# FFN2 of chunks 1 to 8 as a seven-product block multiplication, in an attention-plus-FFN kernel

## The chip, the cores and the metric

One core of one Trainium2 chip. The metric is device time in microseconds (us) of one execution, the median of several; lower is better. Before the change: 338.33 us (337.58 to 338.6, three runs). The profiled executions have a span some 2 us shorter than the timed value, because the span runs from the first to the last instruction.

## The reference, cut to what matters

```python
def reference(q, k, v, w_gate, w_val, w_out):            # shortened
    # q, k, v: 8 batches, 8 heads, 576 positions, head size 64
    attn = softmax(q k^T / 8, masked to |i-j| <= 32) v
    x = attn as [4608 tokens, 512]
    g = x @ w_gate                                       # 512 -> 1536
    val = x @ w_val
    return (g * sigmoid(g) * val) @ w_out                # 1536 -> 512, float32
```

The last line is FFN2, the two lines ahead of it are FFN1. The kernel works through the tokens in nine chunks of 512. Only FFN2 of chunks 1 to 8 is changed.

## The kernel before

FFN1 of a chunk is twelve units. A unit is eight matmuls of 512 columns into one of two `gv_ps` buffers (in PSUM, where matmuls put their results), a silu on ScalarE, and a multiply on VectorE that writes a row of blocks of hT and frees the buffer.

```python
    def ffn1_unit(j, fk):
        ...
        gv = ps_a.tile([128, 2, 512], FP32, tag="a", name="gv_ps")     # ps_a: 2 buffers
        for i, w in enumerate((wg16, wv16)):
            for g in range(GS):
                nc.tensor.matmul(out=gv[:, i, :], lhsT=w[:, g, 128 * fk:128 * fk + 128],
                                 rhs=xts[j][:, g, :], start=(g == 0), stop=(g == GS - 1))
        ssb = spool.tile([128, 512], FP16, tag="s", name="ssb")
        nc.scalar.activation(out=ssb, in_=gv[:, 0, :], func=AF.Silu, bias=0.0, scale=1.0)
        nc.vector.tensor_tensor(out=hts[j][:, fk, :], in0=ssb, in1=gv[:, 1, :], op=ALU.mult)

    def ffn2_sub(j, sub, half=None):                     # 128 tokens, half of the contraction
        ...
        for fk in {None: range(FKS), 0: range(FKS // 2), 1: range(FKS // 2, FKS)}[half]:
            nc.tensor.matmul(out=ob, lhsT=hts[j][:, fk, 128 * sub:128 * sub + 128],
                             rhs=wo16[:, fk, :], start=(fk == 0), stop=(fk == FKS - 1))
        if half == 0:
            return
        osb = opool.tile([128, d_model], FP32, tag="osb", name="osb")
        nc.scalar.activation(out=osb, in_=ob, func=AF.Copy, bias=0.0, scale=1.0)
        nc.sync.dma_start(out=out[r0:r0 + 128, :], in_=osb)
```

FFN2 of a chunk has eight slots (four times 128 tokens, two halves). The attention of the next batch is woven between them, in pieces of 128 tokens (two blocks of 64) that the program calls pairs: scores with exp (ScalarE) and mask (VectorE), then the product with v, a division on VectorE that gives x, and a transpose transfer that gives xT, which FFN1 of the next chunk needs.

```python
        groups = {1: ((), (0, 1)), 3: ((0,), (2, 3)), 5: ((1, 2), (4,)), 7: ((3, 4), ())}
        for slot in range(8):
            at_a, at_s = groups.get(slot, ((), ()))
            done = [todo[i] for i in at_a if i < n]
            for i, m in enumerate(done):
                pair_av(m, ps_a if i else None)          # o_ps on PE, then x on VectorE
            for i in at_s:
                if i < n:
                    pair_scores(todo[i])                 # s_ps on PE, exp on ScalarE, mask on VectorE
            for m in done:
                pair_xt(m)                               # transpose transfer of x
            ...
            ffn2_sub(j, slot // 2, slot % 2)
```

The last 128 tokens of chunk 8 go through `ffn2_last`, in two halves of 256 columns, so that the last output transfer is small.

## Time and profile before

I call the time from the first FFN2 matmul of chunk j to the first FFN1 matmul of chunk j+1 "stage j".

| | us |
|---|---|
| time, median | 338.33 |
| FFN1 of a chunk | 20.7 to 20.9 |
| FFN2 of chunk 7, nothing woven in | 10.36 |
| stages 1 to 6, attention woven in | 13.3 to 14.7 |
| last FFN2 matmul to the end | 5.76 |

The page of the kernel before, its first part (busy time and share of the span by engine), two rows of its second part (busy tenths in 40 equal slices) and its fourth part (the chain of work that ended last):

```profile
span 336.5 us, 6449 instructions
PE 321.8 (96%) x2592; PEld 154.4 (46%) x2592; DVE 157.5 (47%) x289; ACT 155.6 (46%) x222; POOL 106.3 (32%) x139
...
PE   5789998999999999999999999999999999999993
...
DVE  3743366337624763466345644564446634404400
...
PE 87%; DMA 4%; ACT 3%; DVE 3%; issue 1%; SPq 1%; ACTq 0%
PE gv_ps L392 56%; PE ob L406 24%; PE o_ps L354 3%; PE s_ps L306 3%; DMA qk_st<-in_k_dram 2%; DMA xT<-x 2%; ACT xT L262 1%; ACT p_t L312 1%; DVE x L363 1%; PE qk_ps L281 1%; DVE p_t L344 1%; PE ob L425 1%; ACT v L262 1%; SPq L215 0%; PE warm L438 0%
```

TensorE (PE) is the bound from the fifth slice on, so fewer columns through it should be less time. VectorE (DVE) looks half idle.

The groups of instructions of the kernel before, one line for each shape. The columns are line, engine, operation, output and inputs, shapes, count; then busy us and mean ns of one; then the idle time of the engine just before them and what ended it:

```profile
L406 PE MATMUL ob<-wo,hT 128*128 128x512 f16 x420 | 97.3, 380 | 0.0
L399 DVE TENSOR_TENSOR hT<-ssb,gv_ps 128x512 f16<-128x512 f16 x108 | 74.3, 688 | 122.5 <-ACT ssb L398 122.1
L322 DVE TENSOR_TENSOR p_t<-p_t,mask 128x1024 f16<-128x1024 f16 x32 | 22.0, 691 | 14.4 <-ACT p_t L312 14.3
L425 PE MATMUL ob<-wo,hT 128*128 128x256 f16 x24 | 2.8, 272 | 0.0
```

The "380" and "272" are modelled lengths of pipelined matmuls; the pitch is what counts, 216 ns for 512 columns and 109.6 ns for 256 (24 of them in 2.63 us in the chain).

Two more views of the kernel before are needed later. First, who TensorE waited for ahead of FFN1 (line, whom for, us in total, times, longest):

```profile
PE gv_ps L392 <- ACT xT L262: 1.1, 2, 0.7
PE gv_ps L392 <- DMA xT<-x: 0.8, 2, 0.6
```

### The profile page before, as it was taken

How to read it: one execution, taken by the hardware profiler on the slowest of the kernel's cores; microseconds unless marked ns; L12 is line 12 of the kernel's file. 1: busy time of each engine (PE TensorE's matmuls, PEld its weight loads, DVE VectorE, ACT ScalarE, POOL GpSimd, SP SyncE). 2: the span in 40 equal slices, each digit the busy share in tenths (PEclk: the TensorE clock that was granted, in tenths of full speed). 3: DMA queues.
4: the chain of work that ended last, by engine and by line, in shares of the span. 5: the costliest groups of instructions: out<-in, count | busy, mean ns of one | idle time of the engine just before them, and what ended most of it. 6: DMA issues, size and time to landing. Idle time of an engine off the chain costs nothing.

```text
span 336.5 us, 6449 instructions
## 1 busy us (share of the span) xinstructions
PE 321.8 (96%) x2592; PEld 154.4 (46%) x2592; DVE 157.5 (47%) x289; ACT 155.6 (46%) x222; POOL 106.3 (32%) x139
## 2 busy tenths in 40 slices
PE   5789998999999999999999999999999999999993
PEld 2444554444544454445444454454445544444442
DVE  3743366337624763466345644564446634404400
ACT  3864577434543474338333843373337443223321
POOL 8972776148004620364047302560000000000000
PEclk9999999999999999999999999999999999999998
DMA  7999999999959996999599958995530420020012
GB/s 278 161 204 302 217 164 190 153 137 123 128 141 139 112 149 134 131 134 127 158 121 143 117 132 116 153 139 127 120 62 33 111 63 0 34 94 0 2 63 71
DMA packets 152981, 41.92 MB, mean 125 GB/s; under 512 B 140528, under 2 KB 146416, under 8 KB 152944
## 3 DMA queue, kind: packets, MB, share of 16 engines
q0 software_dynamic: 100640, 16.52, 67.2%
q1 hardware_dynamic: 52304, 24.92, 30.6%
q8 instruction: 22, 0.36, 0.5%
q14 instruction: 15, 0.12, 0.1%
HBM read 37.75 MB, written 9.44 MB: 140 GB/s over the span
## 4 chain that ended last, share of the span: by engine, by line
PE 87%; DMA 4%; ACT 3%; DVE 3%; issue 1%; SPq 1%; ACTq 0%
PE gv_ps L392 56%; PE ob L406 24%; PE o_ps L354 3%; PE s_ps L306 3%; DMA qk_st<-in_k_dram 2%; DMA xT<-x 2%; ACT xT L262 1%; ACT p_t L312 1%; DVE x L363 1%; PE qk_ps L281 1%; DVE p_t L344 1%; PE ob L425 1%; ACT v L262 1%; SPq L215 0%; PE warm L438 0%
## 5 line engine op out<-in xcount | busy, mean ns | idle before, releaser
L399 DVE TENSOR_TENSOR hT<-ssb,gv_ps 128x512 f16<-128x512 f16 x108 | 74.3, 688 | 122.5 <-ACT ssb L398 122.1
L398 ACT ACTIVATE ssb<-gv_ps 128x512 f16<-128x512 f32 x108 | 64.5, 597 | 113.2 <-PE gv_ps L392 110.8
L392 PE MATMUL gv_ps<-xT,wg 128*128 128x512 f16 x432 | 110.8, 379 | 1.8 <-ACT xT L262 1.1
L392 PE MATMUL gv_ps<-xT,wv 128*128 128x512 f16 x432 | 110.9, 379 | 0.0
L406 PE MATMUL ob<-wo,hT 128*128 128x512 f16 x420 | 97.3, 380 | 0.0
L392 PEld LDWEIGHTS <-wg 128*128 128x128 f16 x432 | 41.9, 98 | 52.3 <-issue 3.4
L392 PEld LDWEIGHTS <-wv 128*128 128x128 f16 x432 | 42.3, 98 | 51.0
L406 PEld LDWEIGHTS <-hT 128*128 128x128 f16 x420 | 38.5, 98 | 43.7
L223 POOL DMA_DIRECT2D tok<-in_q_dram x30 | 25.2, 841 | 82.0 <-DMA qT<-tok 79.0
L312 ACT ACTIVATE p_t<-s_ps 128x1024 f16<-128x1024 f32 (+1 forms) x40 | 35.4, 935 | 11.2 <-PE s_ps L306 11.1
L414 ACT ACTIVATE osb<-ob 128x512 f32<-128x512 f32 x35 | 21.0, 599 | 39.6 <-PE ob L406 39.6
L223 POOL DMA_DIRECT2D tok<-in_k_dram x30 | 25.2, 839 | 18.7 <-DMA kT<-tok 13.4
L322 DVE TENSOR_TENSOR p_t<-p_t,mask 128x1024 f16<-128x1024 f16 x32 | 22.0, 691 | 14.4 <-ACT p_t L312 14.3
L363 DVE TENSOR_TENSOR x<-o_ps,rall 128x512 f16<-128x512 f32 x36 | 24.9, 692 | 1.2
L242 POOL DMA_DIRECT2D v<-in_v_dram x24 | 21.5, 906 | 0.3 <-PE s_ps L306 0.3
L265 DVE COPY v<-v 64x512 f16<-64x512 f16 x54 | 18.4, 341 | 1.7
L354 PEld LDWEIGHTS <-p_t 128*64 128x64 f16 x576 | 11.2, 110 | 10.4 <-issue 5.9
L354 PE MATMUL o_ps<-v,p_t 128*64 128x66 f16 x576 | 14.0, 196 | 0.7 <-DVE p_t L344 0.7
L361 DVE RECIPROCAL rall<-o_ps 128x8 f32<-128x8 f32 x36 | 7.3, 203 | 14.8 <-PE o_ps L354 14.8
L306 PE MATMUL s_ps<-qT,kT 64*128 64x64 f16 x576 | 12.2, 191 | 0.4 <-DVE kT L265 0.4
L306 PEld LDWEIGHTS <-kT 64*128 64x128 f16 x576 | 9.6, 95 | 5.7 <-issue 3.8
L438 PE MATMUL warm<-mask 128*128 128x512 f16 x26 | 8.3, 439 | 2.9 <-DVE mask L202 2.9
(56 smaller groups left out, 108.1 us busy)
## 6 DMA issues: line engine op xcount, KB each, us to landing
out_dram<-osb SPq DMA_DIRECT2D x35, 256.0 KB, 2.4
v<-in_v_dram POOLq DMA_DIRECT2D x24, 128.0 KB, 5.1
tok<-in_q_dram POOLq DMA_DIRECT2D x24, 128.0 KB, 4.7
tok<-in_k_dram POOLq DMA_DIRECT2D x24, 128.0 KB, 4.9
qk_st<-in_q_dram SPq DMA_DIRECT2D x4, 576.0 KB, 7.2
qk_st<-in_k_dram SPq DMA_DIRECT2D x4, 576.0 KB, 9.0
v<-in_v_dram POOLq DMA_DIRECT2D x16, 96.0 KB, 4.5
wo<-in_moe_w_out_dram POOLq DMA_DIRECT2D x4, 384.0 KB, 21.5
```

Of the source, the lines that this page charges most:

```text
L223: nc.gpsimd.dma_start(out=t[0:n].rearrange("p (h d) -> p h d", d=D), in_=src[b].rearrange("h s d -> s h d")[128 * m:128 * m + n])
L242: nc.gpsimd.dma_start(out=dst[:, 2 * m, :, 0:D], in_=src[128 * m - 32:128 * m + 96])
L306: nc.tensor.matmul(out=s[:, e, c, :], lhsT=kT[b % 2][half, g, 64 * t:64 * t + 128], rhs=qT[b % 2][half, g, 64 * t:64 * t + 64], start=True ...
L312: nc.scalar.activation(out=o, in_=s, func=AF.Exp, bias=0.0, scale=1.0 / float(D) ** 0.5)
L322: nc.vector.tensor_tensor(out=flat, in0=flat, in1=mask, op=ALU.mult)
L354: nc.tensor.matmul(out=o[64 * i:64 * i + 64, h // 4, 66 * (h % 4):66 * (h % 4) + 66], lhsT=p[:, place(b, h)[0], i, place(b, h)[1], :], rhs ...
L363: nc.vector.tensor_tensor(out=x16s[m], in0=ov[:, :, :, 0:D], in1=r.unsqueeze(3).to_broadcast([128, 2, 4, D]), op=ALU.mult)
L392: nc.tensor.matmul(out=gv[:, i, :], lhsT=w[:, g, 128 * fk:128 * fk + 128], rhs=xts[j][:, g, :], start=(g == 0), stop=(g == GS - 1))
L398: nc.scalar.activation(out=ssb, in_=gv[:, 0, :], func=AF.Silu, bias=0.0, scale=1.0)
L399: nc.vector.tensor_tensor(out=hts[j][:, fk, :], in0=ssb, in1=gv[:, 1, :], op=ALU.mult)
L406: nc.tensor.matmul(out=ob, lhsT=hts[j][:, fk, 128 * sub:128 * sub + 128], rhs=wo16[:, fk, :], start=(fk == 0), stop=(fk == FKS - 1))
L414: nc.scalar.activation(out=osb, in_=ob, func=AF.Copy, bias=0.0, scale=1.0)
```

## The change

The contraction of FFN2 (1536) and the 512 output columns are each split in two, and so are the 512 tokens. The eight block products become seven, by the Winograd form of Strassen's scheme. Four sums of h blocks (S1 to S4) are made on VectorE per chunk, four combinations of weight blocks (T1 to T4) once, in FFN1 of chunk 1. The products accumulate in two PSUM tiles (`x`, `y`; in the last chunk also `z`), and the partial results that two outputs share are copied out by ScalarE ("kept") and added by VectorE. Each product is twelve matmuls of 256 columns. The intent: seven eighths of the FFN2 columns on TensorE. To make room in FFN1, the shifts of v move from units 8 to 11 to units 3 to 6.

```diff
-    def ffn2_last(j):
 ...
+    def wino_weights():
 ...
+        sub = lambda o, a, b: nc.vector.tensor_tensor(out=o, in0=a, in1=b, op=ALU.subtract)
+        return [lambda: sub(t3, b22, b12), lambda: sub(t1, b12, b11),
+                lambda: sub(wide, b12, b11), lambda: sub(wide, b22, wide),      # wide is float32
+                lambda: sub(t4, b21, wide),
+                lambda: nc.vector.tensor_copy(out=t2, in_=wide)]
+    def wino_sums(j, lo, hi):
 ...
+        return [lambda: tt(s1, a21, a22, ALU.add), lambda: tt(s2, s1, a11, ALU.subtract),
+                lambda: tt(s3, a11, a21, ALU.subtract), lambda: tt(s4, a12, s2, ALU.subtract)]
 ...
+        def keep_act(name, src):                         # PSUM -> SBUF on ScalarE
+        def total(src, name, i, c, put=True):            # add on VectorE (or copy), then send
 ...
+        def p1():
+            product(x, a(0, 0), b11, True)
+            keep_act("s1", x)
+        def p2():
+            product(y, a(0, 1), b21, True)
+        def c11():
+            total(y, "s1", 0, 0)
+        def p6():
+            product(x, s2, t2, False)
+            keep_act("u2", x)
+        def p5():
+            product(z, s1, t1, True)
+            keep_act("p5", z)
+        def p7():
+            product(x, s3, t3, False)
+            total(x, "p5", 1, 1)
+        def p3():
+            product(z, s4, b22, False)
+            total(z, "u2", 0, 1)
+        def p4():
+            product(x, a(1, 1), t4, False)
+            total(x, None, 1, 0)
 ...
-            if b < B and u in (8, 9, 10, 11):
-                shift_v(b, u - 8, cast_dve)
+            if b < B and u in (3, 4, 5, 6):
+                shift_v(b, u - 3, cast_dve)
+            if j == 1 and u < 6:
+                tw[u]()
+            if u in (8, 9, 10, 11):
+                wino_sums(j, 0, 4)[u - 8]()
 ...
-            if (j, slot) == (NCH - 1, 6):
-                ffn2_last(j)
-                break
-            ffn2_sub(j, slot // 2, slot % 2)
+            if slot < 7:
+                steps[slot]()
+            if slot == 0:
+                for f in late:                           # wino_sums(j, 4, 6)
+                    f()
 ...                                                      # slot 1: mask, c11, mask
```

More of the change, by code (lines that the diff above doesn't have):

```diff
@@ L312, in exp_act, with pair_mask, pair_scores @@
         nc.scalar.activation(out=o, in_=s, func=AF.Exp, bias=0.0, scale=1.0 / float(D) ** 0.5)
-    def pair_scores(m):
+    def pair_mask(m):
+        flat = pts[m].rearrange("p e i g q -> p (e i g) q")
+        nc.vector.tensor_tensor(out=flat, in0=flat, in1=mask, op=ALU.mult)
+    def pair_scores(m, masked=True):
         s = ps_a.tile([128, 2, 8, 64], FP32, tag="a", name="s_ps")
@@ L321, in pair_scores @@
         exp_act(flat, s.rearrange("p e c q -> p (e c) q"))
-        nc.vector.tensor_tensor(out=flat, in0=flat, in1=mask, op=ALU.mult)
+        if masked:
+            pair_mask(m)
     def quad_scores(ms, F):
@@ L416, in ffn2_sub @@
         nc.sync.dma_start(out=out[r0:r0 + 128, :], in_=osb)
-    def ffn2_last(j):
-        r0 = 512 * j + 384
-        for c, (pool, tag) in enumerate(((ps_o, "o"), (ps_c, "c"))):
-            cols = slice(256 * c, 256 * c + 256)
-            ob = pool.tile([128, 256], FP32, tag=tag, name="ob")
-            for fk in range(FKS):
-                nc.tensor.matmul(out=ob, lhsT=hts[j][:, fk, 384:512], rhs=wo16[:, fk, cols],
-                                 start=(fk == 0), stop=(fk == FKS - 1))
-            osb = opool.tile([128, 256], FP32, tag="osb2", name="osb2", bufs=2)
-            if c == 0:
-                cast_act(osb, ob)
-            else:
-                cast_dve(osb, ob)
-            nc.sync.dma_start(out=out[r0:r0 + 128, cols], in_=osb)
+    ws = {}
@@ new lines, in wino_weights @@
+    def wino_weights():
+        top = qkst.tile([128, 3, FKS // 2, 256], FP16, tag="qkst", name="w_top")
+        s3 = qkst.tile([128, 3, FKS // 2, 256], FP16, tag="qkst", name="s_top")
+        rest = qkst.tile([128, 2, FKS // 2, 256], FP16, tag="qkst", name="ws_rest")
+        wide = qkst.tile([128, FKS // 2, 256], FP32, tag="qkst", name="w_wide")
+        wv_ = wo16.rearrange("p (f c) d -> p f c d", c=2)
+        b11, b12 = wv_[:, :, 0, 0:256], wv_[:, :, 0, 256:512]
+        b21, b22 = wv_[:, :, 1, 0:256], wv_[:, :, 1, 256:512]
+        ws["b"] = (b11, b21, b22)
+        ws["t"] = [top[:, 0], top[:, 1], top[:, 2], rest[:, 0]]
+        ws["s"] = [s3[:, 0], s3[:, 1], s3[:, 2], rest[:, 1]]
+        t1, t2, t3, t4 = ws["t"]
+        sub = lambda o, a, b: nc.vector.tensor_tensor(out=o, in0=a, in1=b, op=ALU.subtract)
[3 more added lines that the diff above has]
+                lambda: nc.vector.tensor_copy(out=t2, in_=wide)]
@@ new lines, in wino_sums @@
+    def wino_sums(j, lo, hi):
+        h = hts[j].rearrange("p (f c) q -> p f c q", c=2)[:, lo:hi]
+        a11, a21 = h[:, :, 0, 0:256], h[:, :, 0, 256:512]
+        a12, a22 = h[:, :, 1, 0:256], h[:, :, 1, 256:512]
+        s1, s2, s3, s4 = [t[:, lo:hi] for t in ws["s"]]
+        tt = lambda o, a, b, op: nc.vector.tensor_tensor(out=o, in0=a, in1=b, op=op)
+        return [lambda: tt(s1, a21, a22, ALU.add), lambda: tt(s2, s1, a11, ALU.subtract),
+                lambda: tt(s3, a11, a21, ALU.subtract), lambda: tt(s4, a12, s2, ALU.subtract)]
@@ new lines, in wino_steps, with product, send @@
+    def wino_steps(j, split):
+        h = hts[j].rearrange("p (f c) q -> p f c q", c=2)
+        a = lambda i, c: h[:, :, c, 256 * i:256 * i + 256]
+        b11, b21, b22 = ws["b"]
+        (s1, s2, s3, s4), (t1, t2, t3, t4) = ws["s"], ws["t"]
+        if split:
+            x = [ps_a.tile([128, 256], FP32, tag="a", name="x_ps") for _ in range(2)]
+            y = [ps_o.tile([128, 256], FP32, tag="o", name="y_ps") for _ in range(2)]
+            z2 = ps_c.tile([128, 2, 512], FP32, tag="c", name="z_ps")
+            z = [z2[:, 0, 0:256], z2[:, 1, 0:256]]
+            parts = (0, 1)
+        else:
+            xt = ps_o.tile([128, 2, 256], FP32, tag="o", name="x_ps")
+            yt = ps_o.tile([128, 2, 256], FP32, tag="o", name="y_ps")
+            x, y = [xt[:, 0], xt[:, 1]], [yt[:, 0], yt[:, 1]]
+            z = y
+            parts = (None,)
+        views = lambda t, n: t[n] if split else (xt if t is x else yt)
+        kept = {}
+        def product(dst, lhs, rhs, first):
+            for n in range(2):
+                for f in range(FKS // 2):
+                    nc.tensor.matmul(out=dst[n], lhsT=lhs[:, f, 128 * n:128 * n + 128],
+                                     rhs=rhs[:, f, :],
+                                     start=(first and f == 0 and (split or n == 0)),
+                                     stop=(f == FKS // 2 - 1), skip_group_check=True)
+        def keep_act(name, src):
+            for n in parts:
+                t = kept[(name, n)] = opool.tile([128, 2, 256] if n is None else [128, 256], FP32,
+                                                 tag="kept" if n is None else f"kept{n}",
+                                                 name="kept", bufs=3)
+                cast_act(t, views(src, n))
+        def send(n, o, i, c):
+            r0 = 512 * j + 256 * i + 128 * (n or 0)
+            cols = slice(256 * c, 256 * c + 256)
+            if n is None:
+                nc.sync.dma_start(out=out[r0:r0 + 256, cols].rearrange("(s p) d -> p s d", p=128),
+                                  in_=o)
+            else:
+                nc.sync.dma_start(out=out[r0:r0 + 128, cols], in_=o)
+        def total(src, name, i, c, put=True):
+            for n in parts:
+                o = opool.tile([128, 2, 256] if n is None else [128, 256], FP32,
+                               tag="osb" if n is None else "osb2", name="osb")
+                if name is None:
+                    cast_act(o, views(src, n))
+                else:
+                    nc.vector.tensor_tensor(out=o, in0=views(src, n), in1=kept[(name, n)],
+                                            op=ALU.add)
+                send(n, o, i, c)
+        def p1():
[20 more added lines that the diff above has]
+            total(x, None, 1, 0)
+        return p1, p2, p6, p5, p7, p3, p4, c11
@@ L564 @@
     load_v(2, range(5))
+    tw = wino_weights()
     def ffn1(j):
@@ L587 @@
         n = len(todo)
+        steps = wino_steps(j, j == NCH - 1)
+        late = wino_sums(j, 4, 6)
         groups = {1: ((), (0, 1)), 3: ((0,), (2, 3)), 5: ((1, 2), (4,)), 7: ((3, 4), ())}
@@ L596 @@
                 if i < n:
-                    pair_scores(todo[i])
+                    pair_scores(todo[i], slot > 1)
             for m in done:
                 pair_xt(m)
-            if (j, slot) == (NCH - 1, 6):
-                ffn2_last(j)
-                break
-            ffn2_sub(j, slot // 2, slot % 2)
+            if slot < 7:
[3 more added lines that the diff above has]
+                    f()
+            if slot == 1:
+                for i in at_s[:1]:
+                    if i < n:
+                        pair_mask(todo[i])
+                steps[7]()
+                for i in at_s[1:]:
+                    if i < n:
+                        pair_mask(todo[i])
     fast.close()
```

## The prediction

> **What bounds it now.** TensorE: the page gives PE 321.8 us busy of a 336.5 us span (96%), clock 0.995; the chain of waits is PE for 87% (gv_ps, FFN1, 56%; ob, FFN2, 24%). FFN1 of a chunk takes 20.8 us (twelve units of 1.73). FFN2 alone takes 10.36 us (chunk 7: 48 matmuls of 512 columns, 216 ns each); with the next batch's attention woven in, 13.3 to 14.5 us (chain in order of time). VectorE is 47% busy over all, but 8.4 to 9.3 us within those stages (busy time by stretch).
>
> **Removed.** Seven products for eight: 84 matmuls of 256 columns. The 24 such matmuls ending the kernel now took 2.63 us, 109.6 ns each, weight loads hidden. So 9.2 us instead of 10.36: 1.15 us saved in each of eight chunks, 9.2 us at most.
>
> **Added, on VectorE** (ScalarE still empties four tiles a chunk).
> - Per chunk four sums of 1024 fp16 elements (mask multiply of that form: 691 ns) during FFN1, four of 512 (estimate 0.42 us) after it, three adds from PSUM (hT multiply: 688 ns): 6.5 us.
> - Once, in chunk 1's FFN1, six weight operations of 1536 elements. The Trainium skill, "VectorE: DVE Perf Modes", the perf-mode tier table, lets tensor_tensor run 2x on 16-bit SBUF operands, 1x on fp32 or PSUM; the trace agrees (691 ns for 1024 fp16, 688 for 512 with PSUM). Three touch fp32: 1.76 us each by that page's (N+151)/0.96 (estimate); two 0.95, one 1.1; 8.3 us in all, in units that also get the moved v shifts (0.68 us a unit).
>
> **On the critical path** (estimates from these durations):
> 1. Chunk 1's FFN1: VectorE gets 14 us of work while TensorE does six units in 10.4. Two gv_ps buffers leave 0.4 us of slack; TensorE stalls about 3.7 us, once.
> 2. FFN2 stages 1 to 6: late sums run until 4 us into the stage; exp starts 1.3 us later, behind the first eviction; the first mask ends near 5 us, where TensorE wants it at 4.5: a 0.5 us stall. The second pair of slot 5 gets its x at 11.5 us instead of 10.4 (VectorE full), its transpose needs 2.9 to 4 us more, while TensorE is through at 12.3. Chunks 2 and 3 wait for that x: stages 1 and 2 grow to 14.6 and 15.3 us (from 13.5 and 14.5). Chunks 4 and 5 wait for the pair before: even. Stages 5 and 6 gain 0.9 to 1.0 each.
> 3. Chunks 7 and 8: product three waits for the late sums, in 7 product four for the combine: gain 0.45 and 0.8.
>
> Sum: +3.7 (weights) +1.9 (stages 1, 2) 0 (3, 4) -1.9 (5, 6) -1.25 (7, 8) = +2.5 us.
>
> **Prediction: 340.8 us**, 8 in 10 between 337.0 and 345.0. Faster by over 2%: 0.05; within 2%: 0.85; slower by over 2%: 0.10.
>
> **What would show it.** PE busy falls 9 us, the span does not; PE idle before gv_ps: 3.7 us to hT's multiply in chunk 1, 2 us each to the xT transpose ahead of chunks 2 and 3; before o_ps 0.5 us a stage to the mask; VectorE near 218 us busy, 90% in FFN2 stages 1 and 2; stages 5 and 6 near 12.4 and 12.9 us.
>
> **What would make it wrong.** Weight operations cheaper or hidden: 2 to 4 us come back. Transposes landing later behind output transfers in 1 KB rows, or products waiting for whole tiles of sums: 0.5 us more a stage, nearing +2%. 256-column matmuls not hiding weight loads at length: the saving goes.

## More of the kernel before

Exp and silu need different activation tables on ScalarE, so each chunk with attention woven in switches the table to exp and back to silu. In the trace of the kernel before a table load takes 1283 ns; six stand ahead of that exp and eight ahead of a silu.

Second, the timeline of the kernel before around the start of chunk 2's FFN1 (start us, length us, engine, line, operation; in brackets the idle time before and its releaser):

```profile
95.06 0.60 ACT L414 ACTIVATE osb<-ob 128x512 f32<-128x512 f32 x1 [2.52 <-PE ob L406]
95.12 1.02 PE L392 MATMUL gv_ps<-xT,wg 128*128 128x512 f16 x4 [0.15 <-DMA xT<-x]
95.67 1.28 ACT L398 ACT_TABLE_LOAD   x1
97.05 0.60 ACT L398 ACTIVATE ssb<-gv_ps 128x512 f16<-128x512 f32 x1
```

The table load runs at once after ScalarE's last eviction, while TensorE is still in the first unit. When that unit is done the table is there.

## The result

The changed kernel takes 352.17 us in the median (352.0 to 352.71, four runs, all correct) where the kernel before took 338.47 in the same comparison. The ratio of the means is 1.0417 (95% interval 1.0394 to 1.0441): 4% slower, outside the predicted range. (Ratios here are the mean time of one kernel's runs over that of the other's of the same rounds, so they are not quite the ratio of the medians that I quote.) Executions over 1.5% slower than the fastest of the same kernel are left out of the means.

The page of the changed kernel, first part, the same two rows of the second part:

```profile
span 350.3 us, 7133 instructions
PE 314.7 (90%) x2868; PEld 182.0 (52%) x2868; DVE 210.3 (60%) x385; ACT 155.7 (44%) x226; POOL 107.1 (31%) x139
...
PE   6789998969969998899889998999899989899990
...
DVE  3743475797825785477547783776467834724650
```

TensorE's busy time fell by 7.1 us as intended, and the span grew by 13.8. So TensorE idles 20.9 us more (14.7 before, 35.6 after). The PE row shows where: a notch at every change of stage, which the row of the kernel before does not have, and an empty last slice.

I read the first matmul of every FFN1 and every FFN2 from the two timelines. The differences add up to the 13.8 us of the spans:

| stretch | before, us | after, us | difference | predicted |
|---|---|---|---|---|
| start to FFN1 of chunk 1 | 60.77 | 60.52 | -0.25 | 0 |
| FFN1 of chunk 1 | 20.72 | 24.78 | +4.06 | +3.7 |
| stages 1 and 2 | 28.31 | 29.95 | +1.64 | +1.9 |
| stages 3 and 4 | 27.24 | 27.43 | +0.19 | 0 |
| stages 5 and 6 | 27.24 | 25.87 | -1.37 | -1.9 |
| stage 7 | 10.36 | 10.90 | +0.54 | -0.45 |
| FFN1 of chunks 2 to 7, all six | 124.61 | 131.44 | **+6.83** | **0** |
| FFN1 of chunk 8 | 20.93 | 20.93 | 0 | 0 |
| FFN2 of chunk 8 | 10.56 | 10.03 | -0.53 | -0.8 |
| last matmul to the end | 5.76 | 8.45 | **+2.69** | **0** |
| sum | 336.5 | 350.3 | +13.8 | +2.45 |

What I had costed came out within about 1 us a line, in part because errors cancel within a line: stage 1 grew by 1.84 us (predicted 1.1) and stage 2 fell by 0.20 (predicted +0.8), stage 3 grew by 0.87 and stage 4 fell by 0.68 (predicted even). Two lines that I had not costed at all hold 9.5 of the 11.4 us of the error.

**The weights (size as predicted).** The timeline of the changed kernel in chunk 1's FFN1, VectorE and the matmuls that waited:

```profile
67.13 1.75 DVE L438 TENSOR_TENSOR w_wide<-wo 128x1536 f32<-128x1536 f16 x1
...
69.51 0.61 DVE L265 COPY v<-v 64x512 f16<-64x512 f16 x2
...
70.15 1.76 DVE L438 TENSOR_TENSOR w_wide<-wo,w_wide 128x1536 f32<-128x1536 f16 x1
...
71.82 0.68 DVE L404 TENSOR_TENSOR hT<-ssb,gv_ps 128x512 f16<-128x512 f16 x1
...
72.56 1.02 PE L397 MATMUL gv_ps<-xT,wg 128*128 128x512 f16 x4 [1.14 <-DVE hT L404]
...
73.42 1.76 DVE L438 TENSOR_TENSOR ws_rest<-wo,w_wide 128x1536 f16<-128x1536 f16 x1
...
75.83 1.02 PE L397 MATMUL gv_ps<-xT,wg 128*128 128x512 f16 x4 [1.39 <-DVE hT L404]
```

A shift of v (0.61 us) and a weight operation of 1.76 us delay the hT multiply behind them to 71.82, and with it the release of a gv_ps buffer: TensorE starts again at 72.56, after 1.14 us of idle time. There are four stalls in all. The first, 0.22 us, follows the weight operation of 67.13 alone; ahead of the other three (1.14, 1.39 and 0.68 us) VectorE has a shift of v as well.

**FFN1 of chunks 2 to 7 (not predicted).** The waits of the changed kernel (the same columns as before):

```profile
ACT L403 <- PE gv_ps L397: 16.3, 6, 4.5
PE gv_ps L397 <- DVE hT L404: 9.5, 10, 1.4
...
PE gv_ps L397 <- DMA xT<-x: 5.4, 3, 2.8
```

The first line is new: an instruction of ScalarE at the silu's line, with no tile, waited six times for TensorE's gv_ps. The timeline of the changed kernel at the start of chunk 2's FFN1 shows which it is:

```profile
96.04 0.69 DVE L368 TENSOR_TENSOR x<-o_ps,rall 128x512 f16<-128x512 f32 x1
...
97.67 0.60 ACT L262 ACTIVATE osb<-x_ps 128x512 f32<-128x512 f32 x1 [3.89 <-PE x_ps L478]
...
100.78 1.02 PE L397 MATMUL gv_ps<-xT,wg 128*128 128x512 f16 x4 [2.77 <-DMA xT<-x]
...
102.75 1.28 ACT L403 ACT_TABLE_LOAD   x1 [4.48 <-PE gv_ps L397]
...
104.04 1.09 ACT L403 ACTIVATE ssb<-gv_ps 128x512 f16<-128x512 f32 x2
...
104.67 1.28 DVE L404 TENSOR_TENSOR hT<-ssb,gv_ps 128x512 f16<-128x512 f16 x2 [5.66 <-ACT ssb L403]
...
105.41 1.02 PE L397 MATMUL gv_ps<-xT,wg 128*128 128x512 f16 x4 [1.02 <-DVE hT L404]
```

ScalarE is free at 98.27, but the table load does not start then. It waits until the first unit of FFN1 is complete at 102.7, and only then takes its 1.28 us. The first hT multiply is 1.3 us late, both gv_ps buffers are full, and TensorE stops for 1.02 us ahead of the third unit. This happens in each of the six chunks whose stage switched to exp, and not in chunk 8.

The order of ScalarE's instructions with the semaphores each waits for, as the two programs were built, shows why (a semaphore is the counter by which one engine tells another that work is done; the semaphore numbers in the two traces agree with these lists):

```
before:                                    after:
eviction osb    waits DMA, PE, Activation  eviction osb    waits DMA, DMA, DVE, PE
table load      waits DVE                  table load      waits PE
silu            waits PE                   silu            waits Activation
```

In both programs the first silu has two semaphores to wait for, and one of the two waits is put on the table load ahead of it. Before, that was the one for VectorE, long fulfilled. In the changed program ScalarE has already waited for VectorE earlier in the stage, that wait has become unnecessary, and the load carries the wait for TensorE. That ScalarE's earlier wait is the reason is my reading of the lists; that the load carries the wait for TensorE is what they show.

**Stage 1 (mechanism as predicted, size larger: +1.84 us for +1.1).** In the changed kernel x of the second pair is done at 96.73 and the first FFN1 matmul comes at 100.78, after 2.77 us of idle time that the transpose transfer ended (both in the view above the lists). In the kernel before that idle time was 0.15 us.

**The end (not predicted).** The last instructions of the changed kernel:

```profile
340.38 1.47 PE L478 MATMUL x_ps<-ws_rest,hT 128*128 128x256 f16 x12
340.58 0.78 DVE L506 TENSOR_TENSOR osb<-z_ps,kept 128x256 f32<-128x256 f32 x2 [0.83 <-PE z_ps L478]
341.58 0.38 ACT L262 ACTIVATE osb<-x_ps 128x256 f32<-128x256 f32 x1 [2.96 <-DMA out_dram<-osb]
344.25 0.38 ACT L262 ACTIVATE osb<-x_ps 128x256 f32<-128x256 f32 x1 [2.29 <-DMA out_dram<-osb]
```

The last eviction starts 2.4 us after the last matmul's end, because its output buffer still has to be sent: eight results of the last chunk share three 1 KB buffers. In the kernel before, the answering lines are:

```profile
327.96 2.78 PE L425 MATMUL ob<-wo,hT 128*128 128x256 f16 x24
...
330.78 0.42 DVE L265 COPY osb<-ob 128x256 f32<-128x256 f32 x1 [9.24 <-PE ob L425]
```

### The profile page after: what moved, and what is told of

Read it like the earlier page. It is cut to its first block, busy times and chain, and to the rows that moved or that the text cites. A ratio compares the mean times of both kernels' runs of the same rounds, so it can differ in the third digit from the quotient of the medians.

```text
span 350.3 us, 7133 instructions
## 1 busy us (share of the span) xinstructions
PE 314.7 (90%) x2868; PEld 182.0 (52%) x2868; DVE 210.3 (60%) x385; ACT 155.7 (44%) x226; POOL 107.1 (31%) x139
## 5 line engine op out<-in xcount | busy, mean ns | idle before, releaser
L397 PEld LDWEIGHTS <-wg 128*128 128x128 f16 x432 | 41.5, 98 | 66.2 <-issue 14.6
L223 POOL DMA_DIRECT2D tok<-in_q_dram x30 | 26.1, 869 | 90.1 <-DMA qT<-tok 73.1
L478 PEld LDWEIGHTS <-hT 128*128 128x128 f16 x288 | 27.6, 98 | 5.6 <-issue 0.7
L478 PEld LDWEIGHTS <-s_top 128*128 128x128 f16 x288 | 27.6, 98 | 5.2 <-DVE s_top L450 1.4
L478 PE MATMUL x_ps<-w_top,s_top 128*128 128x256 f16 x192 | 23.8, 273 | 1.2 <-DVE s_top L450 1.2
L265 DVE COPY v<-v 64x512 f16<-64x512 f16 x54 | 20.8, 386 | 1.7
L450 DVE TENSOR_TENSOR s_top<-hT 128x1024 f16<-128x1024 f16 (+1 forms) x32 | 17.6, 551 | 0.0
L403 ACT ACT_TABLE_LOAD x8 | 10.3, 1283 | 16.4 <-PE gv_ps L397 16.3
L359 PE MATMUL o_ps<-v,p_t 128*64 128x66 f16 x576 | 13.8, 196 | 3.8 <-DVE p_t L316 2.2
L262 ACT ACTIVATE osb<-x_ps 128x512 f32<-128x512 f32 (+1 forms) x9 | 4.9, 549 | 25.3 <-PE x_ps L478 20.1
L262 ACT ACTIVATE kept<-x_ps 128x512 f32<-128x512 f32 (+1 forms) x18 | 9.9, 552 | 11.5 <-PE x_ps L478 11.5
```

Source lines behind the costliest of these rows:

```text
L223: nc.gpsimd.dma_start(out=t[0:n].rearrange("p (h d) -> p h d", d=D), in_=src[b].rearrange("h s d -> s h d")[128 * m:128 * m + n])
L265: nc.vector.tensor_copy(out=o, in_=i)
L359: nc.tensor.matmul(out=o[64 * i:64 * i + 64, h // 4, 66 * (h % 4):66 * (h % 4) + 66], lhsT=p[:, place(b, h)[0], i, place(b, h)[1], :], rhs ...
L450: tt = lambda o, a, b, op: nc.vector.tensor_tensor(out=o, in0=a, in1=b, op=op)
L478: nc.tensor.matmul(out=dst[n], lhsT=lhs[:, f, 128 * n:128 * n + 128], rhs=rhs[:, f, :], start=(first and f == 0 and (split or n == 0)), st ...
```

## The experiments

Ten kernels ran, all correct. Those called e1 to e3 and e5 to e8 change one thing in the changed kernel (e5 has e2's edit besides); e4 changes one thing in the kernel before; f1 and f2 combine. "Stage" and FFN1 times are from the profiled execution of each run, medians from the timed ones.

### e1_preload: load the silu table early

```diff
+        if n:                      # at the end of stages 1 to 6
+            nc.scalar.activation(out=dummy, in_=rall[0:1, 0, 0:1], func=AF.Silu, bias=0.0, scale=1.0)
```

> The changed kernel with one 1x1 Silu on ScalarE after the last product of stages 1 to 6, so that the activation table is loaded there, waiting for nothing. Theory (the load carries the first silu's wait for TensorE, so it starts 1.7 us late): the 1.02 us stall of gv_ps in unit 2 of FFN1 of chunks 2 to 7 goes, six times, 6.1 us off: about 346 us, FFN1 of those chunks back to 20.8 us from 21.9. Rival (VectorE is behind at the start of FFN1 because of the combines): the stall stays, 352 us.

Measured: 346.41 us (344.96 to 346.95), ratio to before 1.0238 (1.0209 to 1.0268). That is 5.8 us less than the changed kernel. The timeline of e1_preload at the same place:

```profile
99.73 0.60 ACT L262 ACTIVATE osb<-x_ps 128x512 f32<-128x512 f32 x1 [3.89 <-PE x_ps L478]
...
100.34 1.28 ACT L730 ACT_TABLE_LOAD   x1
...
104.51 0.60 ACT L403 ACTIVATE ssb<-gv_ps 128x512 f16<-128x512 f32 x1 [2.67 <-PE gv_ps L397]
...
105.98 1.03 PE L397 MATMUL gv_ps<-xT,wg 128*128 128x512 f16 x4
```

The load again follows the eviction, the third unit starts without idle time, and FFN1 of chunks 2 to 7 is back at 20.7 us, 7.07 us less in all. (The span fell by 5.5 only: in this profile FFN1 of chunk 1 began 1.7 us later.) VectorE's work was not touched, so the rival falls.

### e4_late_load: bring the stall into the kernel before

```diff
+        if fk == 0 and 2 <= j < NCH - 1:
+            late = const.tile([1, 1], FP32, name="late")
+            nc.scalar.activation(out=late, in_=gv[0:1, 0, 0:1], func=AF.Copy, bias=0.0, scale=1.0)
         nc.scalar.activation(out=ssb, in_=gv[:, 0, :], func=AF.Silu, bias=0.0, scale=1.0)
```

> The kernel before with one 1x1 copy on ScalarE that waits for the first gv_ps of chunks 2 to 7, ahead of the first silu; the table load then comes after that wait, as it does in the changed kernel. Nothing of the seven-product scheme is in it. Theory: 1.0 to 1.3 us of TensorE idle before gv_ps of unit 2 in each of six chunks, 6 to 8 us in all: 345 to 346 us. Rival (VectorE's load is needed for the stall): no change, 338.5 us.

Measured: 345.42 us (345.29 to 347.35), ratio 1.0238 (1.0206 to 1.027). Six copies of one element, 0.16 us each on an engine that is 46% busy in the kernel before, cost 7.4 us. The timeline of e4_late_load:

```profile
96.80 0.16 ACT L400 ACTIVATE late<-gv_ps 1x1 f32<-1x1 f32 x1 [1.40 <-PE gv_ps L392]
96.97 1.28 ACT L401 ACT_TABLE_LOAD   x1
...
98.90 1.29 DVE L402 TENSOR_TENSOR hT<-ssb,gv_ps 128x512 f16<-128x512 f16 x2 [4.58 <-ACT ssb L401]
99.64 0.59 PE L392 MATMUL gv_ps<-xT,wg 128*128 128x512 f16 x2 [1.15 <-DVE hT L402]
```

The same picture without any part of the change. With e1 this shows the cause from both sides: the time at which the table load may start.

### e3_w16: four fp16 weight operations instead of six

```diff
-                lambda: sub(wide, b12, b11), lambda: sub(wide, b22, wide),
-                lambda: sub(t4, b21, wide),
-                lambda: nc.vector.tensor_copy(out=t2, in_=wide)]
+                lambda: sub(t2, b22, t1), lambda: sub(t4, b21, t2)]
-            if j == 1 and u < 6:
+            if j == 1 and u < 4:
```

> The changed kernel with the weight combinations as four fp16 subtractions (about 0.95 us each, units 0 to 3 of chunk 1) instead of six operations of which three take 1.76 us (8.2 us in all). Theory (VectorE work beyond what a unit of 1.73 us has room for stalls TensorE through the two gv_ps buffers): FFN1 of chunk 1 falls from 24.8 us to about 21.5 us, 349 us in all. Rival (the moved v shifts in units 3 to 6 are the cause): still over 23 us.

Measured: 348.98 us (348.12 to 350.16), ratio 1.033 (1.0301 to 1.036). FFN1 of chunk 1 falls from 24.78 to 21.06 us with the shifts of v where the change put them. So the moved shifts alone are not the cause; without the long weight operations one stall of 0.18 us is left. How much these operations would have stalled TensorE without the shifts was not run. The result stays within the comparison's tolerance with the rounded combinations.

### e2_tail and e5_tail_act: the end of the kernel

```diff
 # e2_tail
+            both = opool.tile([128, 2, 256], FP32, tag="osb", name="osb")
             for n in parts:
-                o = opool.tile([128, 2, 256] if n is None else [128, 256], FP32,
-                               tag="osb" if n is None else "osb2", name="osb")
+                o = both if n is None else both[:, n]
 # e5_tail_act, besides
-                nc.sync.dma_start(out=out[r0:r0 + 128, cols], in_=o)
+                q_ = nc.scalar if (i, c) == (1, 0) else nc.sync
+                q_.dma_start(out=out[r0:r0 + 128, cols], in_=o)
```

> The changed kernel with the last chunk's combined blocks written to the three 2 KB output buffers, halves of one tile each, instead of three 1 KB buffers shared by eight results. Theory (the last evictions wait for output transfers to free a buffer): the 2.96 and 2.29 us waits of ScalarE at the end go, and the time from the last matmul to the end falls from 8.6 to about 5.7 us: 349.3 us. Rival (eight output transfers of 128 KB issued one by one on the same queue are the limit, buffers or not): less than 1 us gained.

> The changed kernel with the output buffers of the run e2_tail and, besides, the last product's two transfers issued from ScalarE's queue instead of SyncE's. In e2_tail the waits for a buffer were gone, but the eight issues on SyncE's queue stretched (one took 1.56 us, the last ended 1.9 us after its data was ready). Theory (the issue queue is the second limit behind the buffers): from the last matmul to the end 5.7 us or less instead of 7.6, about 349.5 us. Rival (the transfers themselves are the limit): as e2_tail, 351.5 us.

Measured: e2_tail 351.71 us (350.89 to 353.61), ratio 1.0424 (1.0389 to 1.0458); e5_tail_act 351.83 us (351.05 to 352.15), ratio 1.0407 (1.039 to 1.0425). Neither is told apart from the changed kernel by its time, so both expectations of about 349.5 us were wrong. In e2_tail the waits of ScalarE for a buffer are gone:

```profile
341.08 0.38 ACT L262 ACTIVATE osb<-x_ps 128x256 f32<-128x256 f32 x1 [2.62 <-PE x_ps L478]
341.74 0.38 ACT L262 ACTIVATE osb<-x_ps 128x256 f32<-128x256 f32 x1 [0.27 <-PE x_ps L478]
```

From the last matmul to the end it takes 8.45 us in the profile of the changed kernel, 7.5 in e2_tail and 6.7 in e5_tail_act, against 5.76 before. So the buffers account for perhaps 1 us and the issue queue for less than that, one profile each; the timed runs do not show either gain. The Trainium skill, "Trainium Kernel Development and Optimization", Key Constraints, says that issuing from several engines "only saves the sequencer's issue time"; the 0.8 us between the two profiles do not speak against it. What remains fits another fact that no run isolated: three of the four output blocks of the last chunk leave after the fifth product or later, where the kernel before sent three quarters of its output while it was still multiplying. That part stays open.

### e6_check: the range check after the products of chunk 7

The kernel checks, at the end of chunk 7's FFN1, that all softmax sums are in range. Its five VectorE operations stand ahead of the late sums in the changed program.

```diff
-        if j == NCH - 2:
-            good = check_range()
 ...
+            if slot == 6 and j == NCH - 2:
+                good = check_range()
```

> The changed kernel with the range check's five VectorE operations (1.5 us) after chunk 7's products instead of ahead of the late sums. Theory: product three of chunk 7 waited 1.17 us for the sums behind them, and product four 0.22 us more; stage 7 falls from 11.0 us to 9.7 to 9.9 us, 351 us in all. Rival (the late sums alone make the wait): stage 7 stays above 10.5 us.

Measured (one look): stage 7 takes 9.47 us, where the changed kernel's takes 10.90 and the kernel before takes 10.36. The one time, 351.58 us, is in keeping with that but settles nothing. So stage 7 loses its gain to 1.5 us of VectorE work that cost nothing before: in the kernel before TensorE has no idle time in stage 7.

### e7_xt_pe: transpose the last needed pairs on TensorE

```diff
+            on_pe = {1: (1, 2), 2: (1, 2), 3: (1,)}.get(j, ())
+            if slot == 7:
+                for i in on_pe:
+                    pair_xt(todo[i], True, (ps_a, "a"), cast_dve if i == on_pe[-1] else None)
 ...
-                pair_xt(m)
+                if todo.index(m) not in on_pe:
+                    pair_xt(m)
```

> The changed kernel with the last needed pairs of stages 1 to 3 transposed on TensorE (four 128-column matmuls a pair, 0.3 us) and emptied by ScalarE and VectorE instead of by the transpose transfer. Theory (gv_ps of chunks 2, 3 and 4 waits 2.8, 1.2 and 1.5 us for a transfer that takes about 4 us after x): those waits fall to 1 us or less each, about 3 us off, 349 us. Rival (x itself is late because VectorE is full): TensorE waits for x instead, less than 1 us off.

Measured: 348.84 us (348.73 to 349.3), ratio 1.0319 (1.0302 to 1.0336), 3.3 us less than the changed kernel. Stages 1, 2 and 3 fall from 15.48, 14.47 and 14.19 us to 13.51, 14.01 and 13.07. The timeline of e7_xt_pe ahead of chunk 2:

```profile
96.32 0.69 DVE L368 TENSOR_TENSOR x<-o_ps,rall 128x512 f16<-128x512 f32 x1
...
97.75 0.61 PE L384 MATMUL xt_ps<-ident,x 128*128 128x128 f16 x8
...
99.09 1.02 PE L397 MATMUL gv_ps<-xT,wg 128*128 128x512 f16 x4 [0.35 <-ACT xT L262]
```

TensorE did not wait for x itself; the transfer was what it waited for, once the stage had become shorter than x plus the transfer.

### e8_exp: load the exp table early

```diff
+        if n:                      # after the last silu of FFN1, ahead of product one's eviction
+            nc.scalar.activation(out=dummy, in_=rall[0:1, 0, 0:1], func=AF.Exp, bias=0.0, scale=1.0)
```

> The changed kernel with a 1x1 exp on ScalarE after the last silu of FFN1, so that the exp table is loaded while product one runs and not behind its eviction. Theory (the 0.45 us stall of o_ps in six stages comes from exp starting behind eviction and load): the exps start 0.6 to 0.7 us earlier and the stall goes, 2.7 us off, 349.5 us. Rival (VectorE with its late sums is what holds the mask): the stall stays at 0.3 us or more.

Measured: 348.98 us (348.33 to 349.63), ratio 1.0313 (1.0296 to 1.0331), 3.2 us less than the changed kernel. The 0.45 us of idle time ahead of o_ps is gone in all six stages, and stages 4, 5 and 6 fall from 13.24, 12.64 and 13.23 us to 12.72, 12.12 and 12.72.

### f1_all and f2_old_last: all remedies together

f1_all has the edits of e1, e3, e5 (with e2's), e6, e7 and e8. f2_old_last leaves chunk 8's FFN2 as it was before the change:

```diff
+        if j == NCH - 1:
+            for slot in range(6):
+                ffn2_sub(j, slot // 2, slot % 2)
+            ffn2_last(j)
+            break
```

> The changed kernel with all remedies together: both table loads early, fp16 weight combinations, the last results in the larger buffers with two issue queues, the range check late, transposes of the last needed pairs on TensorE. Adding up what each took off alone (5.8 + 3.2 + 0.4 + 1.4 + 3.4 + 3.2 = 17.4 us): about 335 us, 1% faster than the kernel before. From the stage times that the traces of the single runs gave (stages 1 to 8 about 12.7, 13.3, 12.4, 12.7, 12.1, 12.7, 9.5, 9.9 us, FFN1 20.7 each) it would be 331 us. If the seven-product scheme as such costs TensorE more than it saves, it stays above 338 us.

> As f1_all, but the last chunk is multiplied in eight products as in the kernel before, with its evictions. Theory (three quarters of the last chunk's output leave after product five and lengthen the tail by more than the saved product is worth there): the last stage 10.5 us instead of 9.9, the tail 5.7 us instead of 6.9: about 0.6 us faster than f1_all. Rival (the tail is a matter of issue and chance): 0.5 us slower.

Measured: f1_all 332.38 us (330.4 to 335.06, six runs), ratio 0.9823 (0.9784 to 0.9862); f2_old_last 332.07 us (330.98 to 335.31, six runs), ratio 0.98 (0.9775 to 0.9826), with the kernel before at 338.55 us. Both beat both kernels, the one before by about 1.8 to 2% and the changed one by some 20 us. That they are faster than the kernel before is clear of the noise; that they are so by 2% is not. f1_all lies between the two figures expected of it, 335 and 331 us. The page of f1_all, first part and the PE row of the second:

```profile
span 330.0 us, 7148 instructions
PE 314.5 (95%) x2888; PEld 183.6 (56%) x2888; DVE 205.9 (62%) x386; ACT 158.9 (48%) x240; POOL 106.5 (32%) x139
...
PE   6789999999999999999999999999999999999992
```

The notches are gone. TensorE's busy time is that of the changed kernel (314.7 us); now the span has followed it. From the first FFN1 matmul of chunk 1 to the last matmul TensorE idles 0.75 us in the kernel before, 19.6 in the changed one and 1.5 in f1_all. So the seven-product scheme does what it was meant to do on TensorE, and what it lost was lost to waits. It also rules out that the remedies did it without the scheme: in that stretch of the kernel before they had at most 0.75 us to win.

f1 and f2 are not told apart: their intervals overlap. In the profile, FFN2 of chunk 8 and what follows it take 16.6 us in f1_all, 16.4 in f2_old_last and 16.3 in the kernel before: in the last chunk the scheme gains nothing. Both kernels scatter more than the one before (1.4% from lowest to highest, against 0.6%). The profiled execution of f2_old_last, its slowest, has a wait that the others do not have:

```profile
PE gv_ps L397 <- DMA xT<-x: 2.1, 1, 2.1
```

It stands ahead of chunk 6; the longest such wait in the kernel before was 0.6 us. The clock adds to it: the first matmul after the wait starts at 230.94, and from 231.6 on the granted TensorE clock is 0.50 for 3.4 us, and FFN1 of chunk 6 takes 22.40 us where it takes 20.73 in f1_all. The wait and the slow clock together are some 3.8 us of this run. The profiles of e3, e6 and e8 show the same 3.4 us at 0.50 at the start of chunk 2's FFN1, after waits of 2.5 us. The changed kernel idles 2.77 us at that place without it, so the length of the wait alone does not decide. In the timed runs the slowest execution of f1_all and of f2_old_last has the lowest mean clock of its kernel (0.989 and 0.990; the fastest 0.998 and 0.997). That these two things are the cause of all the scatter is not shown.

## Why the prediction was wrong

- **TensorE's saving: right.** Products come 1.31 us apart (twelve matmuls, 109 ns each, weight loads hidden); TensorE's busy time fell by 7.1 us where I said 9. Busy time is partly modelled: a group of twelve matmuls is shown as 1.47 us at a pitch of 1.31, so each interruption adds some 0.16 us to it.
- **Weights in chunk 1: right.** 3.7 us predicted, 4.06 measured, and e3 takes all but 0.34 us of it away. The float32 operations took 1.75 and 1.76 us, as the formula of the Trainium skill, "VectorE: DVE Perf Modes", the section on the TRN2 errata, gave them.
- **Stages 1 to 6: mechanism right, sizes by stage mixed.** x of the second pair was done 11.4 us into stage 1 (predicted 11.5), TensorE was through at about 12.7 (12.3), the transfer took 4.05 us more (2.9 to 4). The stall ahead of o_ps was 0.45 us in each of six stages (0.5), and e8 shows its cause. But stage 1 took 15.48 us where I had 14.6, and stage 2 14.47 where I had 15.3: TensorE waited 2.77 us ahead of chunk 2 and 1.17 ahead of chunk 3, where I had said 2 each. That their sum came out near (+1.64 for +1.9) is luck. Stage 3 lost 0.87 us and stage 4 gained 0.68, where I had both even: the wait for the transfer reached one chunk further than I thought (1.49 us ahead of chunk 4). Stages 5 and 6 took 12.64 and 13.23 us (predicted 12.4 and 12.9).
- **Step 2 and the sum, wrong: a term left out.** The sum goes from stage to stage and takes FFN1 of chunks 2 to 7 as unchanged; step 2 says only that "exp starts 1.3 us later, behind the first eviction" and names no table load. So the start of exp is in it, and the switch back to silu is not. That term was +6.83 us in the trace; e1 takes 5.8 us of the time away, and e4 makes 7.4 us of it in the kernel before. No line of the diff touches the silu. The term came from which semaphore wait the build put on the table load; that this changed because other waits on ScalarE changed is my reading and was not run by itself.
- **Step 3 and the sum, wrong: the end left out.** I took the tail as before; it grew by 2.69 us. I had read the buffer count of the evictions (three) and not counted the eight results that now share them. The waits were the buffers' (e2), but the time hardly fell when they were gone, so most of this term is not settled. In the single profiles FFN2 of chunk 8 and what follows take 18.5 us in the changed kernel, 16.8 in e5_tail_act and 16.3 before.
- **Step 3, chunk 7, mis-sized.** Predicted -0.45, measured +0.54 us. I had not put the range check's 1.5 us on VectorE ahead of the sums; with it moved (e6) the stage takes 9.47 us, a gain of 0.9.
- **Signs to look for.** VectorE was to be 90% busy in stages 1 and 2; it was 70% and 82% (10.90 of 15.48 us, 11.91 of 14.47), and both stages ended in a wait for a transfer. Sums that last 0.42 us each started 0.34 us apart (87.79, 88.13 and 88.47), so the lengths of single operations, added up, overstate VectorE's load a little. Its 210.3 us in all were near the 218 predicted.

Of the error of 11.4 us, 6.8 us are the table load, 2.7 the end, 1.0 stage 7; the rest is spread.

## What to carry to other kernels

When TensorE is 96% busy, a change that gives it less work can make every other engine's latencies visible, as here: trace each hand-over (buffer release, table load, transfer) at the new, earlier time at which TensorE will ask for it, in the stages the diff does not touch as well. Where an activation table is switched between stages, load it with a tiny activation at a place of your choice, so that the load cannot inherit a wait from the first real use. When such a change comes out slower, look for TensorE's idle time stage by stage before giving it up: here 352.2 us became 332.4 us with small edits that left the products alone.

## What the Trainium skill lacked or had wrong

- "ScalarE: Activation LUTs", What ACT_TABLE_LOAD costs: the load took 1283 ns here as the page states, but the page adds a drain of about 1380 ns to every switch; here the silu began 0.01 us after the load's end (load at 102.75 for 1.28 us, silu at 104.04). No such drain stood between the two, and none ahead of the load where nothing held it (in e1_preload the eviction ended at 100.33 and the load began at 100.34).
- No page says that the wait of an activation can be put on the table load ahead of it. "Perfetto Trace Analysis", Identifying Dependency Chains, says only that instructions which wait for several engines may get semaphore instructions ahead of them. Here the load took the wait for TensorE, at 1.02 us of idle TensorE each time, six times.
- I found no figure, in "DMA: Bandwidth & Descriptors" or elsewhere, for how much longer a transpose transfer can take to be issued in one place than in another: from x to the matmul that needs xT it took about 3 us ahead of chunk 2 in the kernel before (92.08 to 95.12) and 4.05 us in the changed kernel, at the same size. The difference is in the issue on SyncE's queue, 1.21 us before and 2.15 after; from the end of the issue to the matmul it took 1.35 and 1.42 us.
